# Three early moves in a gated attention and MLP kernel: a load of x onto ScalarE's queue, another load ahead of a transpose, and one key product a place later

## The chip, the cores and the metric

The kernel runs on one core of a Trainium2 chip. A core has TensorE (matrix products, in the profile PE, its weight loads PEld), VectorE (DVE), ScalarE (ACT), GpSimd (POOL) and SyncE (SP), each with an instruction stream of its own, and 16 DMA engines that all of them give work to. Products land in PSUM, eight banks of 512 float32 columns for 128 partitions. The metric is the time on the device in microseconds (us), as a median of several runs; less is better.

## The reference

x has 2048 tokens of 640 features (bfloat16). A gate mixes a linear attention block and an MLP block that both start from x:

```python
def _A_ref(x, wqkv, wo):
    H = 32; Dh = D // H
    qkv = (x @ wqkv).reshape(B, S, 3, H, Dh).transpose(2, 0, 3, 1, 4)
    q, k, v = qkv[0], qkv[1], qkv[2]
    phi = lambda t: jnp.where(t > 0, t + 1, jnp.exp(t)) + 1e-6
    pq, pk = phi(q), phi(k)
    kv = jnp.einsum("bhsd,bhse->bhde", pk, v)
    z = jnp.einsum("bhsd->bhd", pk)
    o = jnp.einsum("bhqd,bhde->bhqe", pq, kv) / (jnp.einsum("bhqd,bhd->bhq", pq, z)[..., None] + 1e-6)
    return o.transpose(0, 2, 1, 3).reshape(B, S, D) @ wo
...
g = _sigmoid((x * gate_w).sum(-1, keepdims=True))
return g * _A_ref(x, wqkv, wo) + (1 - g) * _B_ref(x, w1, w2, w3, w4)
```

`_B_ref` is a layer norm, a 640 by 640 product with GELU, shifts of the tokens by one or two, another 640 by 640 product with a residual, then a second layer norm and an MLP of width 1728 with a residual. The change touches the first stage alone, in which queries and keys are made from x.

## The kernel before, in words

The tokens are 16 tiles of 128. In the first stage each tile of x is loaded (`x_tok`), transposed into `xT`, and multiplied with the query weights `wq` and the key weights `wkg`; ScalarE takes the exponential, and VectorE makes the feature map `phi` of it (a minimum, then a `scalar_tensor_tensor` that reads the product's bank and frees it). The key product carries 130 more columns: the last key features, a column of ones, and the gate.

Instructions are recorded by `_Sched`. It keeps one program for each engine, in the order of recording, and works out the waits from what each instruction reads and writes. `sch.dma("sp", ...)` and `sch.dma("act", ...)` put a DMA into SyncE's or ScalarE's program. An engine works its program in order, so a DMA that waits holds up every later one in that program, its own data's or not.

Tiles 0 to 2 are transposed by TensorE (`t_x`), since nothing else is there to do yet. Tiles 3 to 15 are transposed by DMA: `x_turn(t)` (lines 711 and 712) is a DMA transpose in SyncE's program that waits for the load of its tile; four semaphores are used in turn for these, so turn 7 also waits for turn 3. All loads of x are in SyncE's program too (`load_x`, lines 702 and 703, and the loop at lines 735 to 738). The order there is: loads 0 and 1, one query weight block, loads 2 and 3 (3 waits for 1), turn 3, loads 4 and 5, turns 4 and 5, the load of tiles 6 to 9 as one transfer, turns 6 to 8, the load of tiles 10 to 15, turns 9 to 15. ScalarE's program has four query weight blocks, five key weight blocks (`load_wk`, one for each 128 rows) and the last 128 columns of the query weights, and then its activations.

TensorE's order in the first stage is written out by hand. `q_three` (line 950) interleaves the queries of tiles 0 to 2 with their transposes, `k_three` (line 959) does the keys of the same three tiles: its list has pairs (tile, row block), so (2, 0) is the third tile's product with the first block of 128 weight rows. One such pair is two matmuls, of 512 and 130 columns (lines 943 and 614 in the profile). `stream` issues them; each tile has its pair of PSUM banks for the whole of `k_three`, and the third tile's pair was used by a query before. Behind them each tile from 3 on has its query (`q_tile`, line 606 in the profile), its key (`k_tile`, line 625) and at times a product with all four tiles of a group (`q_turned`) or a step of a product of x and the keys (`gt_tail`). The rest of the kernel, from 54 us on, is ordered by a planner (`_Items.run`) that works with estimated times; its order of instructions and its PSUM banks are the same in both kernels.

Of the kernel before, what the change touches and what calls it, by code (L numbers as in the profile page):

```python
# [15 lines left out]
NT = S // 128  # L16
# [400 lines left out]
def _build(nc, A_x, A_wqkv, A_wo, B_w1, B_w2, B_w3, B_w4, gate_w, out, dbg=None, stop=None):  # L417
    sch = _Sched(nc)
# [54 lines left out]
    x_tok = pa.alloc("x_tok", [128, NT, D], BF16)  # L473
# [46 lines left out]
    def bank():  # L520
        best = None
        for k_ in range(nbanks[0]):
            b = (bank_rr[0] + k_) % nbanks[0]
            if b in bank_pend or b in bank_hold:
                continue
            lk = sch.locks.get(b)
            tfree = 0.0 if lk is None else sch.ev_time.get((lk[1].sem, lk[1].val), 1e18)
            if best is None or tfree < best[0]:
                best = (tfree, b)
        bank_rr[0] = best[1] + 1  # L530
        bank_pend.add(best[1])
        return best[1]
# [4 lines left out]
    def pair():  # L537
        best = None
        for k_ in range(4):
            q_ = (bank_rr[0] // 2 + k_) % 4  # L540
            tf = 0.0
            ok = True
            for b in (2 * q_, 2 * q_ + 1):
                if b in bank_pend or b in bank_hold:
                    ok = False
                lk = sch.locks.get(b)
                if lk is not None:
                    tf = max(tf, sch.ev_time.get((lk[1].sem, lk[1].val), 1e18))
            if ok and (best is None or tf < best[0]):
                best = (tf, 2 * q_)  # L550
        b = best[1]
        bank_rr[0] = b + 2
        bank_pend.update((b, b + 1))
        return b
# [3 lines left out]
    def slot(name, n):  # L558
        i = slot_ctr.get(name, 0)
        slot_ctr[name] = i + 1  # L560
        return i % n
# [49 lines left out]
    def mm_kept(e, o, l, r, start, stop, check=True):  # L611

        ll = e.lower_ap(l, for_matmul_weights=True)
        return e.add_instruction(mybir.InstMatmult(  # L614
            name=nc.get_next_instruction_name(), engine=e.engine, ins=[e.lower_ap(r), ll], outs=[e.lower_ap(o)],
            start_tensor_calc=start, stop_tensor_calc=stop, bass_skip_group_check=not check, tile_size=(128, 128),
            tile_position=(0, 0), ldweights=False))
# [23 lines left out]
    def ts(engf, out_ap, in_ap, s1, s2, op0, op1, extra_reads=()):  # L641
        rd = [in_ap] + [a for a in (s1, s2) if not isinstance(a, (int, float)) and a is not None] + list(extra_reads)
        cost = None
        if engf is pool:
            cost = 190.0 + 1.15 * nfree(out_ap)
        elif in_ap.dtype == BF16 and out_ap.dtype == BF16 and not in_psum(in_ap):
            cost = 65.0 + nfree(out_ap) / 3.84
        return engf(lambda e: e.tensor_scalar(out_ap, in_ap, s1, s2, op0, op1), rd, [out_ap], cost=cost)  # L648
# [9 lines left out]
    def stt(out_ap, in0, scalar, in1, op0, op1, accum=None):  # L658
        rd = [in0, in1] + ([scalar] if not isinstance(scalar, (int, float)) else [])
        n = nfree(out_ap)  # L660
        cost = (65.0 + n / 0.96) if (in_psum(in0) or in_psum(in1)) else (160.0 + 1.04 * n)
        if accum is not None:
            return dve(lambda e: e.scalar_tensor_tensor(out_ap, in0, scalar, in1, op0, op1, accum_out=accum), rd,  # L663
                       [out_ap, accum], cost=cost + 70.0)
        return dve(lambda e: e.scalar_tensor_tensor(out_ap, in0, scalar, in1, op0, op1), rd, [out_ap], cost=cost)  # L665
# [3 lines left out]
    def activation(out_ap, in_ap, func, scale=1.0, bias=0.0, accum=None):  # L669
        rd = [in_ap] + [a for a in (scale, bias) if not isinstance(a, (int, float))]  # L670
        wr = [out_ap] + ([accum] if accum is not None else [])
        n = nfree(out_ap)
        cost = max(150.0, 100.0 + 0.833 * n + (70.0 if in_psum(in_ap) else 0.0)) + 45.0 * (len(rd) - 1)
        if accum is not None:
            cost += 91.0
        st_ = ACT_SET.get(func)
        if st_ is not None and st_ != sch.act_func:
            cost += 1290.0
            sch.act_func = st_
        if accum is not None:  # L680
            return act(lambda e: e.activation(out_ap, in_ap, func, bias=bias, scale=scale, accum_out=accum), rd, wr, cost=cost)  # L681
        return act(lambda e: e.activation(out_ap, in_ap, func, bias=bias, scale=scale), rd, wr, cost=cost)  # L682
# [14 lines left out]
    x2 = A_x[0]  # L697

    def dma_in(out_ap, in_ap, key, **kw):
        return sch.dma("sp", out_ap, in_ap, key, **kw)  # L700

    def load_x(t, **kw):
        dma_in(x_tok[:, t, :], x2[128 * t:128 * (t + 1), :], "x%d" % t, **kw)
# [7 lines left out]
    def x_turn(t):  # L711
        sch.dma("sp", xT[:, :, 128 * t:128 * (t + 1)], x_tok[:, t, :], "trx%d" % (t % 4), transpose=True)
# [14 lines left out]
    sch.dma("act", wq[:, :, 512:D], A_wqkv[:, 512:D].rearrange("(k p) f -> p k f", p=128), "wqt")  # L727
    load_x(3, deps=[sch.dma_last["x1"]])
    sch.dma("pool", xn[0:KD, 1, 0:128], gate_w.rearrange("(k p) -> k p", p=128), "gw")
    x_turn(3)  # L730
    load_x(4)
    load_x(5)
    x_turn(4)
    x_turn(5)
    for t0, t1, turns in ((6, 10, range(6, 9)), (10, NT, range(9, NT))):
        dma_in(x_tok[:, t0:t1, :], x2[128 * t0:128 * t1, :].rearrange("(n p) d -> p n d", p=128), "xc%d" % t0)
        for t in turns:
            x_turn(t)

    k_done = {}  # L740
# [67 lines left out]
    def phi(b, dst, after_exp=None, n=D):  # L808
        se = slot("E", 3)
        src = psf[:, 512 * b:512 * b + n]  # L810
        er = Er[:, se, 0:n]
        activation(er, src, ACTF.Exp)
        if after_exp is not None:
            after_exp()
        ts(dve, er, er, 1.0, EPS_PHI, ALU.min, ALU.add)
        return stt(dst, src, 1.0 + EPS_PHI, er, ALU.add, ALU.max)
# [78 lines left out]
    def warmup(cols, cyc):  # L895
        b = bank()
        one = nc.const_aps.tensor(1.0, [128, 512], BF16)
        steps = [512] * (cols // 512) + [128] * (cols % 512 // 128)

        def fn(e):  # L900
            ins = None
            for n in steps:
                ins = e.matmul(ps[:, b, 0:n], one[:, 0:128], one[:, 0:n], start=True, stop=True)
            return ins
        pe(fn, [], [ps[:, b, :]], cost=cols * cyc)
# [19 lines left out]
    def stream(order, w, n2, done):  # L925
        bs = {}
        for t in sorted({t for t, k in order if k is not None}):
            if not n2 and t == 1:
                bank_rr[0] += 1
            bs[t] = pair() if n2 else bank()  # L930
            bank_hold.update((bs[t], bs[t] + 1) if n2 else (bs[t],))
        for t, k in order:
            if k is None:
                if t is None:
                    warmup(256, 0.42)
                else:
                    t_x(t)
                continue
            b = bs[t]
            l = xT[:, k, 128 * t:128 * (t + 1)]  # L940

            def fn(e, l=l, b=b, k=k):
                ins = e.matmul(ps[:, b, 0:512], l, w[:, k, 0:512], start=(k == 0), stop=(k == KD - 1))
                return ins if not n2 else mm_kept(e, ps[:, b + 1, 0:n2], l, w[:, k, 512:512 + n2], k == 0, k == KD - 1)
            pe(fn, [l, w[:, k, 0:512 + n2]], [ps[:, b, 0:512]] + ([ps[:, b + 1, 0:n2]] if n2 else []), cost=272.0 if n2 else 216.0)
            if k == KD - 1:
                bank_hold.difference_update((b, b + 1) if n2 else (b,))
                done(t, b)

    def q_three():  # L950
        order = [(0, 0), (1, None), (0, 1), (1, 0), (1, 1), (0, 2), (1, 2), (0, 3), (1, 3), (2, None), (0, 4), (1, 4),
                 (2, 0), (2, 1), (2, 2), (2, 3), (2, 4)]
        stream(order, wq, 0, lambda t, b: phi(b, pq_tok[:, t + 1, 0:512], n=512))

    def k_out(t, b):
        k_done[t] = phi(b, pk_tok[:, t, :], lambda: activation(lr[:, t, :], ps[:, b + 1, 128:130], ACTF.Copy))
        activation(junk[:, 0, :], x_tok[:, t, :], ACTF.Square, accum=st1[:, 1, t:t + 1])

    def k_three():
        stream([(0, 0), (1, 0), (2, 0), (0, 1), (1, 1), (0, 2), (2, 1), (1, 2), (0, 3), (2, 2), (0, 4), (1, 3), (2, 3),  # L960
                (1, 4), (2, 4)], wkg, 130, k_out)

    def addA(name, dur, fn, deps=()):
# [461 lines left out]
    for t in range(NT):  # L1425
        g = GOF[t]
        t0, t1 = GROUPS[g]
# [73 lines left out]
```

## Time and profile before

| | us |
|---|---|
| median of 3 runs | 259.33 |
| lowest, highest | 258.81, 259.79 |
| the profiled execution's own time | 259.23 |
| its span, first instruction to last | 258.0 |
| TensorE busy in it | 252.8 |
| ScalarE, VectorE, GpSimd busy | 107.3, 145.2, 91.0 |

Times in the rows are microseconds from the start of the span. In a timeline a row gives the start, the time taken, the engine, the line of the kernel (of a helper, where one records the instruction), the operation, what is written and read, how many were merged, and in brackets how long the engine had been idle and what ended that. "SPq" and "ACTq" rows are the issuing of DMAs, in SyncE's and ScalarE's programs; the transfer itself ends later, and the rows of the DMA view give the median time from issue to landing. A row of waits gives the engine, its line and what it waited for, with the sum, the count and the longest.

### The profile page before, as it was taken

To read this page: it belongs to the slowest core of one execution; us is meant where nothing else is said; L and a number is where in the kernel's file an instruction comes from. 1 tells how busy PE (TensorE), PEld (TensorE's weight loads), DVE (VectorE), ACT (ScalarE), POOL (GpSimd) and SP (SyncE) were. 2 spreads that over 40 slices of the span, in tenths; PEclk is the share of its full clock that TensorE was granted. 3 is DMA by queue.
4 is the path that set the end of the run, shared out by engine and by line. 5 is a ranking of instruction groups with operands and counts; after the bars stand their busy time and mean duration, and the time that the engine had idled before them with its cause. 6 is when DMAs were issued, how large, how long until landed. Compare 5 with 4: busy or idle time off the path is not lost.

```text
span 258.0 us, 3580 instructions
## 1 busy us (share of the span) xinstructions
PE 252.8 (98%) x1392; PEld 110.4 (43%) x1242; DVE 145.2 (56%) x290; ACT 107.3 (42%) x220; POOL 91.0 (35%) x146
## 2 busy tenths in 40 slices
PE   8998999999999999999999999999999999999997
PEld 3333343344444333334444444444444444444444
DVE  2597888899953995589999603759100033200033
ACT  2495676751356858666655600003520100253000
POOL 5021399967772153758919001223000021300000
DMA  6953799845843599462585400032100022200002
GB/s 196 236 152 80 204 172 211 213 105 127 105 101 79 97 335 381 88 103 51 127 104 125 106 10 20 0 127 53 26 0 0 20 24 101 102 1 3 0 20 102
DMA packets 57825, 26.48 MB, mean 103 GB/s; under 512 B 49188, under 2 KB 56397, under 8 KB 57808
## 3 DMA queue, kind: packets, MB, share of 16 engines
q1 hardware_dynamic: 54544, 21.38, 35.8%
q0 software_dynamic: 1168, 3.28, 5.2%
q10 hardware_dynamic: 2096, 1.61, 2.0%
q8 instruction: 10, 0.16, 0.3%
q14 instruction: 7, 0.06, 0.1%
HBM read 12.04 MB, written 2.62 MB: 57 GB/s over the span
## 4 chain that ended last, share of the span: by engine, by line
PE 89%; DMA 7%; SPq 2%; issue 1%; DVE 0%
PE ps L606 35%; PE ps L1238 30%; PE ps L625 11%; PE ps L830 7%; DMA x_tok<-in_A_x_dram 6%; PE ps L614 4%; SPq L281 1%; PE ps L1284 1%; DMA xT<-x_tok 1%; PE ps L1144 1%; PE ps L1030 0%; DVE Mt L691 0%; SPq L285 0%; PE ps L1056 0%; DVE x_tok L665 0%
## 5 line engine op out<-in xcount | busy, mean ns | idle before, releaser
L606 PE MATMUL ps<-xnT,w 128*128 128x512 bf16 x352 | 79.9, 379 | 0.5 <-issue 0.2
L665 DVE SCALAR_TENSOR_TENSOR x_tok<-ps,stg,abx 128x512 bf16<-128x512 f32 (+2 forms) x17 | 12.2, 719 | 78.4 <-PE ps L1238 78.3
L682 ACT ACTIVATE h2T<-ps 128x512 bf16<-128x512 f32 x52 | 30.7, 597 | 59.8 <-PE ps L606 59.8
L606 PEld LDWEIGHTS ps<-xnT,w 128*128 128x128 bf16 x360 | 34.6, 98 | 41.6 <-issue 1.9
L1238 PE MATMUL ps<-w,h2T 128*128 128x512 bf16 (+2 forms) x218 | 45.9, 366 | 0.3 <-issue 0.2
L648 POOL TENSOR_SCALAR xn<-x_tok,st 128x640 bf16<-128x640 bf16 x32 | 34.8, 1093 | 26.1 <-DMA xnT<-xn 25.5
L648 POOL TENSOR_SCALAR abx<-x_tok,stg 128x640 f32<-128x640 bf16 (+1 forms) x16 | 15.0, 944 | 71.2 <-DVE x_tok L665 71.2
L1238 PEld LDWEIGHTS ps<-w,h2T 128*128 128x128 bf16 x221 | 21.1, 98 | 24.1 <-issue 0.3
L682 ACT ACTIVATE Er<-ps 128x512 bf16<-128x512 f32 (+1 forms) x36 | 23.0, 651 | 16.3 <-PE ps L614 10.9
L681 ACT ACTIVATE junk<-x_tok 128x640 bf16<-128x640 bf16 x32 | 23.6, 738 | 3.9 <-DVE x_tok L663 3.7
L682 ACT ACTIVATE hsT<-ps 128x512 bf16<-128x512 f32 (+1 forms) x32 | 19.0, 594 | 13.5 <-PE ps L606 13.1
L625 PE MATMUL ps<-w,hsT 128*128 128x512 bf16 x76 | 22.3, 379 | 0.0
L663 DVE SCALAR_TENSOR_TENSOR x_tok<-ps,x_tok 128x640 bf16<-128x640 f32 x16 | 13.1, 821 | 10.7 <-PE ps L614 10.1
L1238 PE MATMUL ps<-M_sb,pqnT 128*128 128x512 bf16 (+2 forms) x83 | 18.6, 366 | 0.1
L625 PE MATMUL ps<-wkg,xT 128*128 128x512 bf16 x62 | 18.6, 379 | 0.1
L614 PE MATMUL ps<-wkg,xT 128*128 128x130 bf16 x80 | 17.6, 220 | 0.2
L830 PE MATMUL ps<-pk_tok,x_tok 128*128 128x512 bf16 x79 | 17.7, 379 | 0.1
L614 PE MATMUL ps<-w,hsT 128*128 128x128 bf16 x80 | 17.5, 219 | 0.2
L1173 DVE TENSOR_TENSOR pq_tok<-pq_tok,dnr 128x300 bf16<-128x300 bf16 (+1 forms) x48 | 17.2, 412 | 0.5
L648 DVE TENSOR_SCALAR Er<-Er 128x512 bf16<-128x512 bf16 (+1 forms) x36 | 12.3, 341 | 8.0 <-ACT Er L682 7.4
L606 PE MATMUL ps<-wq,xT 128*128 128x512 bf16 x64 | 15.9, 379 | 0.7 <-DMA xT<-x_tok 0.7
L656 DVE TENSOR_TENSOR qprod<-qprod,pk_tok 128x640 f32<-128x640 f32 x13 | 15.2, 1166 | 0.4
(91 smaller groups left out, 252.7 us busy)
## 6 DMA issues: line engine op xcount, KB each, us to landing
w<-in_B_w_dram SPq DMA_DIRECT2D x1, 2160.0 KB, 8.2
w<-in_B_w_dram SPq DMA_DIRECT2D x1, 2080.0 KB, 13.4
out_dram<-x_tok SPq DMA_DIRECT2D x3, 640.0 KB, 3.1
w<-in_B_w_dram POOLq DMA_DIRECT2D x8, 160.0 KB, 4.9
x_tok<-in_A_x_dram SPq DMA_DIRECT2D x6, 160.0 KB, 3.0
x_tok<-in_A_x_dram SPq DMA_DIRECT2D x1, 960.0 KB, 5.5
wkg<-in_A_wqkv_dram ACTq DMA_DIRECT2D x5, 160.0 KB, 3.8
wv<-in_A_wqkv_dram POOLq DMA_DIRECT2D x1, 800.0 KB, 5.2
```

What stands on the lines that cost most here:

```text
L606: ins = e.matmul(out_ap, l, r, start=(i == 0), stop=(i == n - 1))
L614: return e.add_instruction(mybir.InstMatmult(name=nc.get_next_instruction_name(), engine=e.engine, ins=[e.lower_ap(r), ll], outs=[e.lower_ ...
L625: e.matmul(outs[0], l, r, start=st, stop=sp, skip_group_check=True)
L648: return engf(lambda e: e.tensor_scalar(out_ap, in_ap, s1, s2, op0, op1), rd, [out_ap], cost=cost)
L656: return engf(lambda e: e.tensor_tensor(out_ap, a, b_, op), [a, b_], [out_ap], cost=cost)
L663: return dve(lambda e: e.scalar_tensor_tensor(out_ap, in0, scalar, in1, op0, op1, accum_out=accum), rd, [out_ap, accum], cost=cost + 70.0)
L665: return dve(lambda e: e.scalar_tensor_tensor(out_ap, in0, scalar, in1, op0, op1), rd, [out_ap], cost=cost)
L681: return act(lambda e: e.activation(out_ap, in_ap, func, bias=bias, scale=scale, accum_out=accum), rd, wr, cost=cost)
L682: return act(lambda e: e.activation(out_ap, in_ap, func, bias=bias, scale=scale), rd, wr, cost=cost)
L830: ins = e.matmul(o, l, r, start=(t0 + q_ == 0), stop=(t0 + q_ == NT - 1))
L1173: dve(lambda e, o=o, i0=i0, i1=i1: e.tensor_tensor(o, i0, i1, ALU.mult), [i0, dnr[:, 1, sd, :]], [o], cost=cost)
L1238: ins = e.matmul(o, l, r, start=first and i == 0, stop=last and i == len(prs) - 1, skip_group_check=True)
```

## The change

Three things are moved, and nothing is computed differently.

- The load of tiles 6 to 9 (640 KB) goes from SyncE's program to ScalarE's, where it is recorded behind the queries of tiles 0 to 2, that is, behind their third exponential. It has no wait there. Turns 6 to 8, the load of tiles 10 to 15 and turns 9 to 15 keep their order in SyncE's program.
- The load of tile 4 stands ahead of turn 3 in SyncE's program, right behind the load of tile 3.
- In `k_three` the pairs (2, 0) and (0, 1) change places. The wait for the second key weight block moves forward with (0, 1), the wait for VectorE moves back with (2, 0).

```diff
+    load_x(4)
     x_turn(3)
-    load_x(4)
     load_x(5)
     x_turn(4)
     x_turn(5)
-    for t0, t1, turns in ((6, 10, range(6, 9)), (10, NT, range(9, NT))):
-        dma_in(x_tok[:, t0:t1, :], x2[128 * t0:128 * t1, :].rearrange("(n p) d -> p n d", p=128), "xc%d" % t0)
-        for t in turns:
+
+    def load_xs(queue, t0, t1):
+        sch.dma(queue, x_tok[:, t0:t1, :], x2[128 * t0:128 * t1, :].rearrange("(n p) d -> p n d", p=128), "xc%d" % t0)
+
+    def late_x():
+        load_xs("act", 6, 10)
+        for t in (6, 7, 8):
+            x_turn(t)
+        load_xs("sp", 10, NT)
+        for t in range(9, NT):
             x_turn(t)
...
         stream(order, wq, 0, lambda t, b: phi(b, pq_tok[:, t + 1, 0:512], n=512))
+        late_x()
...
-        stream([(0, 0), (1, 0), (2, 0), (0, 1), (1, 1), (0, 2), (2, 1), (1, 2), (0, 3), (2, 2), (0, 4), (1, 3), (2, 3),
+        stream([(0, 0), (1, 0), (0, 1), (2, 0), (1, 1), (0, 2), (2, 1), (1, 2), (0, 3), (2, 2), (0, 4), (1, 3), (2, 3),
                 (1, 4), (2, 4)], wkg, 130, k_out)
```

## The prediction

> **What bounds the kernel now.** I read the page's head and its chain of waits first, then TensorE's waits alone, then the chain of the first 24 us, then the timeline around each place that the change touches.
>
> ```profile
> span 258.0 us, 3580 instructions
> PE 252.8 (98%) x1392; PEld 110.4 (43%) x1242; DVE 145.2 (56%) x290; ACT 107.3 (42%) x220; POOL 91.0 (35%) x146
> ...
> PE 89%; DMA 7%; SPq 2%; issue 1%; DVE 0%
> ```
>
> TensorE is busy for 98% of the span and holds 89% of the chain. The 9% of DMA and SyncE must be one early stretch, since TensorE has few waits of its own:
>
> ```profile
> PE ps L903 <- PEq L1486: 0.8, 1, 0.8
> PE ps L606 <- DMA xT<-x_tok: 0.7, 1, 0.7
> PE ps L606 <- issue: 0.2, 1, 0.2
> PE ps L1238 <- issue: 0.2, 1, 0.2
> ```
>
> The first row is the launch. The second is the only wait for another's work that is listed after it, and the chain of the first 24 us says what it was for:
>
> ```profile
> 4.31 3.60 DMA x_tok<-in_A_x_dram
> ...
> 7.93 1.30 SPq L281
> ...
> 9.28 2.98 DMA x_tok<-in_A_x_dram
> ...
> 14.86 5.77 DMA x_tok<-in_A_x_dram
> ...
> 20.64 2.37 DMA xT<-x_tok
> ...
> 23.05 1.04 PE ps L606 x4
> ```
>
> SyncE's queue works in order. It waits for tile 3 and turns it (7.93), issues tiles 4 and 5 (9.28), waits for them and turns them, and only at 14.86 issues the load of tiles 6 to 9. That lands at 20.63, tile 6 is turned by 23.01, and the query of tile 6 starts at 23.05. What TensorE loses there is read from starts, because a matmul's shown duration overlaps the next one:
>
> ```profile
> 22.14 0.22 PE L614 MATMUL ps<-x_tok,pk_tok 128*128 128x128 bf16 x1
> 23.05 1.25 PE L606 MATMUL ps<-wq,xT 128*128 128x512 bf16 x5 [0.69 <-DMA xT<-x_tok]
> ...
> 29.52 0.22 PE L614 MATMUL ps<-x_tok,pk_tok 128*128 128x128 bf16 x1
> 29.57 1.24 PE L606 MATMUL ps<-wq,xT 128*128 128x512 bf16 x5
> ```
>
> The same pair of instructions follows at 0.05 us two tiles later, and at 0.91 us here. The wait costs 0.86 us, not the 0.69 that is listed as idle.
>
> The second place is the third key tile's first product:
>
> ```profile
> 8.13 0.10 PEld L943 LDWEIGHTS ps<-wkg,xT 128*128 128x128 bf16 x1 [0.15 <-DMA wkg<-in_A_wqkv_dram]
> 8.31 0.38 PE L943 MATMUL ps<-wkg,xT 128*128 128x512 bf16 x1
> 8.33 0.69 DVE L665 SCALAR_TENSOR_TENSOR pq_tok<-ps,Er 128x512 bf16<-128x512 f32 x1
> ...
> 8.58 0.38 PE L943 MATMUL ps<-wkg,xT 128*128 128x512 bf16 x1
> ...
> 9.07 0.33 PEld L943 LDWEIGHTS ps<-wkg,xT 128*128 128x128 bf16 x2 [0.45 <-DVE pq_tok L665]
> 9.08 0.39 PE L943 MATMUL ps<-wkg,xT 128*128 128x512 bf16 x1
> 9.36 0.38 PE L943 MATMUL ps<-wkg,xT 128*128 128x512 bf16 x1
> ```
>
> Products of this stage start 0.27 apart (8.31, 8.58). The third should start at 8.85 and starts at 9.08, because its bank is freed by VectorE at 9.02 (8.33 + 0.69). This loss is 0.23 us.
>
> **The change, part by part.** *The load of tiles 6 to 9* leaves SyncE's queue, and with it the waits for tiles 3, 4 and 5. It is issued by ScalarE behind three exponentials, without a wait of its own.
>
> ```profile
> 7.37 1.73 ACT L682 ACTIVATE Er<-ps 128x512 bf16<-128x512 f32 x3 [3.19 <-PE ps L943]
> 11.74 0.70 ACT L682 ACTIVATE Er<-ps 128x640 bf16<-128x640 f32 x1 [2.64 <-PE ps L614]
> 14.86 0.58 SPq L285 DMA_DIRECT2D x_tok<-in_A_x_dram  x1
> 16.17 1.24 PE L606 MATMUL ps<-wq,xT 128*128 128x512 bf16 x5
> ```
>
> ScalarE is free at 9.10 and next needed at 11.74. One issue of this load took SyncE 0.58, so it ends near 9.7, inside the 2.64 idle: cost nothing. Queued behind it on ScalarE is the first key's exponential, on which VectorE and then TensorE's banks wait; without that idle it would cost up to its 0.58. By its own 5.77 the load lands near 14.9 instead of 20.63. SyncE's queue before turn 6 then holds the load of tile 5 at 9.28 and turns 4 and 5, the latter from about 12.3 (9.28 + 2.98). Turn 6 goes at about 14.9 and lands 2.37 later, at 17.3, against 22.19 where TensorE wants it (22.14 + 0.05). Even with a further 1.2 us (two 160 KB loads in front of it, at the rate in the rows below) the margin is over 3 us. The load of tiles 10 to 15 stays on SyncE behind turn 8, so it moves forward with it. The 0.86 us is gone: I take all of it.
>
> *Tile 4 ahead of turn 3.* SyncE issues it when it is done with tile 3's load, at 4.64 instead of 9.28, and so in the middle of the key weights, which ScalarE issues from 4.57 on:
>
> ```profile
> 2.18 2.46 SPq L285 DMA_DIRECT2D x_tok<-in_A_x_dram  x2
> 4.57 2.27 ACTq L285 DMA_DIRECT2D wkg<-in_A_wqkv_dram  x5
> ...
> 7.00:8.00 1.00, 1.00 (x6) 0.42 (x5) 0.64 (x4) 0.63 (x2) 0.00 (x0) 1.00 1.02 323
> 8.00:9.00 1.00, 1.00 (x7) 0.19 (x2) 0.96 (x3) 0.95 (x2) 0.00 (x0) 1.00 0.79 252
> ...
> 12.00:13.00 1.00, 1.00 (x8) 0.45 (x5) 0.49 (x2) 1.00 (x3) 0.00 (x0) 1.00 0.03 9
> ```
>
> The columns behind the clock are the DMA engines' share and GB/s. From 7 to 9 us they are full or nearly so, so 160 KB more there push what is behind them by 0.5 (323 GB/s) to 0.63 us (252). Who is behind them is seen from the issues, each asked for in its own stretch: the second key weight block (issued at 5.02, 4.57 and a fifth of 2.27) and turn 3 (7.93).
>
> ```profile
> wkg<-in_A_wqkv_dram ACTq DMA_DIRECT2D x1, 160.0 KB, 3.5
> xT<-x_tok SPq DMA_TRANSPOSE x1, 3.8
> ```
>
> The second block landed at 8.52 (5.02 + 3.5). The first, whose row reads the same, landed at 8.07 (4.57 + 3.5), and 8.13 shows its wait ending with TensorE at its own pace of 0.27 behind it, so there is little to spare, but whatever this delays is counted once with the second block's delay.
>
> *The order of the key products.* The second product of tile 0 now stands third, and needs the second block; the one that waits for VectorE stands fourth, at 9.12 at the earliest, behind 9.02. Undisturbed, the second block is there at 8.52, the third product starts at 8.85 and 0.23 is gained. Pushed by 0.63 it lands at 9.15 and is used at 9.21 (the first block's 0.06 from landing to weight load), 0.13 after 9.08: a loss of 0.13. Tile 4 follows tile 3 on SyncE's queue, tile 3 landed at 7.91 (4.31 + 3.60), and so tile 4 takes only a share of the engines before the second block is through. I take a push of 0.4 us: start 8.98, gain 0.10. The ends, -0.13 and +0.23, go into the range.
>
> The Trainium skill, "DMA: Bandwidth & Descriptors", section "Queues, rings and completion order", has each DMA engine take turns, packet by packet, between the queues that have work. By that alone tile 4 would get half of the engines until it is through, and the sum would move by less than the two ends just given.
>
> *Turn 3* landed at 11.73 (7.93 + 3.8) and is first used here:
>
> ```profile
> 12.58 0.80 PEld L606 LDWEIGHTS ps<-wq,xT 128*128 128x128 bf16 x5 [0.17 <-issue]
> ...
> 24.53 0.58 SPq L285 DMA_DIRECT2D x_tok<-in_A_x_dram  x1
> 25.16 1.24 SPq L281 DMA_TRANSPOSE xT<-x_tok  x1
> ...
> xT<-x_tok SPq DMA_TRANSPOSE x1, 6.2
> ```
>
> It has 0.85 us to spare. With weights pushed into it by 0.4 to 0.63 it still comes in time. But the 640 KB now start behind 9.10, while it is under way. The dearest turn of the trace is tile 9's, issued at 25.16 right behind the load of tiles 10 to 15 (960 KB) on its own queue: 6.2 us, the last row. At that price turn 3 lands at 14.13, 1.55 late. The 640 KB are on another queue, behind the last key and query weights, so I stay near the 3.8 and take 0.05 as a mean loss; 0 and 1.55 are the ends. Turn 4 goes at 9.86 (9.28 and an issue of 0.58), and even at 6.2 lands at 16.06, against 16.17.
>
> *What moves later.* VectorE's and GpSimd's instructions, banks and order are the same in both kernels, and behind 23.05 TensorE waits for nobody by the list above. So a shift at 23 us arrives at the end whole.
>
> *Sum:* 0.86 + 0.10 - 0.05 = 0.91 us. The profiled execution took 259.23 us for its span of 258.0. That gives 258.32, and 258.42 from the median of 259.33, which is 0.10 above the profiled one. I say **258.4**.
>
> **Rivals.**
>
> *A, everything at its best:* the second block isn't pushed, 0.86 + 0.23 = 1.09, 258.2. For it: from 8 to 9 us the engines are at 0.79, not full. Against it: 1.02 the microsecond before.
>
> *B, the gain is eaten by the weights:* tile 4 pushes the blocks by the full 0.63 (loss 0.13), and turn 3, pushed by that and by a part of the 640 KB, comes some 0.4 late: 0.86 - 0.53 = 0.33, 259.0. For it: 0.85 is all that turn 3 has.
>
> *C, slower:* turn 3 is crowded as tile 9's was. From 0.85 us of delay on it costs TensorE its excess, from 1.71 on (0.85 + 0.86) it costs more than the change saves, and at 6.2 us it is 1.55 late. With the weights' 0.13 that is 0.86 - 1.68 = -0.82, so 260.1; to pass 260.6 it would have to land 0.5 later still. For it: its data flow while the DMA engines are at their fullest. Against: the large load has a queue of its own here, and stands in it behind 960 KB of weights.
>
> *D, no difference:* the load is issued earlier, but shares the engines so long that tile 6 comes no earlier. Then 0.86 stays lost, and with the order's 0.10 less turn 3's 0.05 the time is 259.3. Against it speaks the window from 12 to 13 us, with the engines at 0.03: there is room for 640 KB before 15 us, and the load was late for its issue's sake. The Trainium skill, "DMA: Bandwidth & Descriptors", section "Rules for kernel authors", says so of every such move: spreading loads over several issuing engines gives no bandwidth, since all run on the same 16 DMA engines, and saves only issue time. The trace agrees that the engines are shared, but the time between 9.3 and 14.86 was spent in SyncE's queue.
>
> **How the numbers follow.** Forecast 0.55, A 0.25, B 0.10, C 0.05, D 0.05. Three runs of before lie from 258.81 to 259.79, so a median moves by some 0.4 either way. Forecast and A with that reach from 257.8 to 258.9, and B and D to 259.4: the range is **257.7 to 259.4**, with C and half of D's upper side left out. About 0.5% (1.3 us, 258.03 and 260.63) is what a measurement of this kernel tells from no change. The forecast stands 0.4 on the slow side of the lower bound, A 0.2: a sixth of the one and a half of the other give 0.09 + 0.13 = 0.22 for faster. Slower takes C whole and a little for what I haven't seen: 0.06. Same is the rest, 0.72.
>
> **What would show it.** TensorE's wait for the turned tile at line 606 is gone, and the load of tiles 6 to 9 stands on ScalarE's queue near 9.1 with turn 6 issued by about 16. The third key product starts between 8.85 and 9.21, and waits for key weights, if for anything. The query of tile 3 follows its key products at 0.05; a wait for the turned tile there is C or B. VectorE's bank wait (9.07) is gone or small. I am wrong if the query of tile 6 still waits, if a new wait on TensorE behind 23 us takes the gain back, or if the three places are as said and the span isn't 0.7 to 1.1 shorter.

## The result, and the profile after

| | before | after |
|---|---|---|
| median, us | 258.94 | 260.88 |
| lowest, highest | 258.49, 259.79 | 258.88, 265.51 |
| runs | 22 | 22 |
| ratio, 95% interval | | 1.0055 (1.0035 to 1.0076) |
| profiled execution's own time | 259.23 | 263.71 |
| its span | 258.0 | 262.5 |

The change makes the kernel slower by 0.35 to 0.76%, and it makes it unsteady: the runs of before lie within 1.3 us, those of after within 6.6. The profiled execution is one of two in 22 in which TensorE's mean granted clock is below 1 (0.993 here; 0.987 in the run of 265.51), and the ratio leaves these two out; a second profile of the same kernel, with a whole clock, follows in the experiments.

The head of the profile's page after, and the chain's shares by engine:

```profile
span 262.5 us, 3580 instructions
PE 254.7 (97%) x1392; PEld 110.7 (42%) x1242; DVE 145.3 (55%) x290; ACT 107.5 (41%) x220; POOL 90.9 (35%) x146
...
PE 92%; DMA 6%; issue 1%; DVE 0%; SPq 0%
```

TensorE still bounds the kernel, but 7.8 us of the span are now without it (262.5 - 254.7), where it was 5.2. TensorE's waits after say for what:

```profile
PE ps L606 <- DMA xT<-x_tok: 3.2, 1, 3.2
PE ps L910 <- PEq L1494: 0.8, 1, 0.8
```

One wait at the same line as before, for a turned tile, but more than four times as long (3.2 against 0.7). The chain of the first 30 us after (start, length, what) says that it is another tile:

```profile
4.49 3.79 DMA x_tok<-in_A_x_dram
8.30 8.03 DMA xT<-x_tok
16.37 1.46 PE ps L606 x5
```

The load of tile 3 ends at 8.28, its turn is issued at 8.30 and lands 8.03 later, at 16.33. So it is turn 3 that the query of tile 3 waits for, not turn 6 any more. The timeline after, with the engines concerned (line 950 of the changed kernel is line 943 of the one before):

```profile
8.15 0.29 DVE L648 TENSOR_SCALAR Er<-Er 128x512 bf16<-128x512 bf16 x1 [0.32 <-ACT Er L682]
8.30 1.29 SPq L281 DMA_TRANSPOSE xT<-x_tok  x1
7.52 1.77 ACT L682 ACTIVATE Er<-ps 128x512 bf16<-128x512 f32 x3 [3.33 <-PE ps L950]
8.70 0.39 ACTq L285 DMA_DIRECT2D x_tok<-in_A_x_dram  x1
...
8.65 0.33 PEld L950 LDWEIGHTS ps<-wkg,xT 128*128 128x128 bf16 x2 [0.50 <-DMA wkg<-in_A_wqkv_dram]
8.94 0.38 PE L950 MATMUL ps<-wkg,xT 128*128 128x512 bf16 x1
9.49 0.33 PEld L950 LDWEIGHTS ps<-wkg,xT 128*128 128x128 bf16 x2 [0.51 <-DMA wkg<-in_A_wqkv_dram]
9.49 0.39 PE L950 MATMUL ps<-wkg,xT 128*128 128x512 bf16 x1
...
12.89 0.33 DVE L648 TENSOR_SCALAR Er<-Er 128x640 bf16<-128x640 bf16 x1 [1.87 <-ACT Er L682]
12.99 0.22 PE L614 MATMUL ps<-wkg,xT 128*128 128x130 bf16 x1
16.37 1.46 PE L606 MATMUL ps<-wq,xT 128*128 128x512 bf16 x5 [3.16 <-DMA xT<-x_tok]
17.63 0.63 PE L625 MATMUL ps<-wkg,xT 128*128 128x512 bf16 x1
18.16 0.63 PE L625 MATMUL ps<-wkg,xT 128*128 128x512 bf16 x1
```

The query of tile 3 should follow the last key product by 0.05, at 13.04, and starts at 16.37: 3.33 us lost. Behind that its key products stand 0.53 apart instead of 0.27. The windows after (length, busy time of the five engines, granted clock, DMA share, GB/s) show why:

```profile
17.30:20.70 3.40, 3.40 (x13) 0.91 (x7) 0.99 (x2) 0.75 (x2) 0.00 (x0) 0.50 0.74 101
20.70:24.00 3.30, 3.25 (x19) 1.31 (x14) 2.53 (x6) 2.41 (x6) 1.91 (x5) 1.00 0.51 107
```

For 3.4 us the granted clock is 0.50, which costs an estimated 1.7 us, half of that stretch. In the first stage, then, the bill against the profile of before reads as follows. The first query's minimum on VectorE starts at 8.15; before, this row and that of the first key stood so (the timeline of before):

```profile
8.00 0.29 DVE L648 TENSOR_SCALAR Er<-Er 128x512 bf16<-128x512 bf16 x1 [0.36 <-ACT Er L682]
12.48 0.33 DVE L648 TENSOR_SCALAR Er<-Er 128x640 bf16<-128x640 bf16 x1 [1.60 <-ACT Er L682]
...
26.80 0.82 DVE L665 SCALAR_TENSOR_TENSOR pk_tok<-ps,Er 128x640 bf16<-128x640 f32 x1
```

So 0.15 is late at the first query (8.15 - 8.00), 0.26 is lost between the two minima (12.89 - 8.15 = 4.74 instead of 4.48), 3.33 in the wait for turn 3, 1.70 by the half clock, and 0.86 is won back, since tile 6 has no wait: 4.58, and the span is longer by 4.5. The same product of VectorE that starts at 26.80 above starts 4.49 later after:

```profile
31.29 0.82 DVE L665 SCALAR_TENSOR_TENSOR pk_tok<-ps,Er 128x640 bf16<-128x640 f32 x1
```

From there to the end of the span the shift stays 4.5 us. All that happened did so in the first 26 us.

Where the 8 us of turn 3 went is seen in the DMA view after. Asked for in their own stretch, the issues of ScalarE's load and of turn 3 (KB, us to landing), and behind them the queues' packets that began from 9 to 10 us, from 10 to 11 and from 13 to 14 (packets, MB, share of 16 engines):

```profile
x_tok<-in_A_x_dram ACTq DMA_DIRECT2D x1, 640.0 KB, 7.7
xT<-x_tok SPq DMA_TRANSPOSE x1, 8.0
...
q10 hardware_dynamic: 467, 0.34, 103.5%
...
q10 hardware_dynamic: 483, 0.15, 80.8%
q1 hardware_dynamic: 241, 0.06, 28.0%
...
q10 hardware_dynamic: 199, 0.25, 82.7%
q1 hardware_dynamic: 199, 0.05, 27.8%
```

q10 carries what ScalarE issues, q1 what SyncE issues. From 9 to 10 us, behind its issue at 8.30, turn 3 has no packet at all; the weights of ScalarE's queue run. From 10 to 11 it gets 241 of its 640 (160 KB in packets of 256 bytes). The rest runs beside the 640 KB. From 13 to 14 us the two queues got 199 packets each, but a packet of the load has 1280 bytes and one of a transpose 256: 0.25 MB went to the load and 0.05 to SyncE's queue, with the turn for which TensorE was standing still. The equal count is that of this one microsecond; from 11 to 12 it was 71 to 121, from 14 to 15 163 to 264.

### The profile page after: what moved, and what is told of

Its sections match the earlier page's. It is cut to its first block, busy times and chain, and to the rows that moved or that the text cites. A ratio compares the mean times of both kernels' runs of the same rounds, so it can differ in the third digit from the quotient of the medians.

```text
span 262.5 us, 3580 instructions
## 1 busy us (share of the span) xinstructions
PE 254.7 (97%) x1392; PEld 110.7 (42%) x1242; DVE 145.3 (55%) x290; ACT 107.5 (41%) x220; POOL 90.9 (35%) x146
## 4 chain that ended last, share of the span: by engine, by line
PE 92%; DMA 6%; issue 1%; DVE 0%; SPq 0%
PE ps L606 37%; PE ps L1246 30%; PE ps L625 13%; PE ps L837 7%; PE ps L614 4%; DMA xT<-x_tok 3%; DMA x_tok<-in_A_x_dram 3%; PE ps L1292 1%; PE ps L1152 1%; PE ps L1038 0%; DVE Mt L691 0%; SPq L285 0%; PE ps L1064 0%; DVE x_tok L665 0%
## 5 line engine op out<-in xcount | busy, mean ns | idle before, releaser
L625 PE MATMUL ps<-wkg,xT 128*128 128x512 bf16 x62 | 19.9, 399 | 0.1
```

Of the source, the lines that this page charges most:

```text
L625: e.matmul(outs[0], l, r, start=st, stop=sp, skip_group_check=True)
```

## The experiments

The theory is that the second queue does the harm: on ScalarE's queue the 640 KB run beside turn 3 and take every other packet, where on SyncE's they would stand behind it. The first rival is that tile 4's early load, and with it the key weights, crowd turn 3. A second is that the amount alone matters, wherever it is issued. Where the expectations use letters, L and O are the theory, W is the first rival and E the second. Diffs are against the changed kernel, those of no_load, order_only and the last pair against the kernel before, that of pool_tile4_back against pool_after_turn3. All medians stand beside those of before that were measured with them:

| kernel | median (range), us | before | ratio (95%) |
|---|---|---|---|
| load_only | 259.17 (258.62 to 262.54) | 259.06 | 1.0026 (1.0000 to 1.0052) |
| no_load | 259.04 (258.66 to 259.55) | 259.06 | 1.0004 (0.9992 to 1.0015) |
| order_only | 259.06 (258.60 to 259.84) | 259.06 | 1.0001 (0.9990 to 1.0013) |
| pool_after_turn3 | 259.17 (258.61 to 259.68) | 259.06 | 1.0004 (0.9992 to 1.0015) |
| own_queue_gone | 259.06 (258.81 to 259.42) | 259.08 | 1.0005 (0.9996 to 1.0014) |
| act_tile6_only | 259.21 (259.04 to 259.62) | 259.08 | 1.0009 (0.9999 to 1.0020) |
| pool_tile4_back | 259.81 (259.25 to 260.00) | 259.08 | 1.0032 (1.0021 to 1.0043) |
| tile6_alone | 258.75 (258.13 to 259.41) | 259.08 | 0.9991 (0.9981 to 1.0002) |
| act_tiles6_7 | 259.59 (258.75 to 260.67) | 259.16 | 1.0016 (1.0002 to 1.0030) |
| tile6_old_order | 258.85 (258.59 to 259.00) | 259.16 | 0.9989 (0.9979 to 0.9998) |

**The parts alone.** *load_only* is the change without tile 4's move and without the key products' order:

```diff
-    load_x(4)
     x_turn(3)
+    load_x(4)
...
-        stream([(0, 0), (1, 0), (0, 1), (2, 0), (1, 1), (0, 2),
+        stream([(0, 0), (1, 0), (2, 0), (0, 1), (1, 1), (0, 2),
```

> Only the load of tiles 6 to 9 is moved to ScalarE's queue; tile 4's load and the key order are as before. Theory L (the 640 KB run on a queue of their own beside turn 3 and hold it up): turn 3 takes over 5.5 us from issue to landing, TensorE's query of tile 3 waits 1 to 3.5 us for it, and the time is 259.5 to 263 with a wide spread from run to run. Rival W (tile 4's early 160 KB push the weights and turn 3; the large load is harmless): turn 3 lands within 4.5 us, no wait there, tile 6's wait is gone, and the time is 258.1, which is 0.86 under the kernel before.

Most of its runs are as before, but 4 of 12 lie above 260 (260.07, 260.49, 260.75, 262.54), and none of before does. The profiled one (258.62) is the shortest. Its timeline and its DMA view:

```profile
8.98 0.42 ACTq L285 DMA_DIRECT2D x_tok<-in_A_x_dram  x1
...
x_tok<-in_A_x_dram ACTq DMA_DIRECT2D x1, 640.0 KB, 4.8
xT<-x_tok SPq DMA_TRANSPOSE x1, 3.4
```

Turn 3 was issued at 7.60 here, 0.7 earlier than after, and took 3.4; no wait at tile 3 is listed. So the profile is as W expected and the spread as L did, and neither foresaw the median. That the load alone does the harm in the four long runs is likely, but none of them has a profile. With tile 4 ahead of turn 3 long runs are the rule: 15 of 22 of the changed kernel are above 260.

*no_load* is the other half, tile 4's move and the order, with the 640 KB left on SyncE's queue:

```diff
+    load_x(4)
     x_turn(3)
-    load_x(4)
...
-        stream([(0, 0), (1, 0), (2, 0), (0, 1), (1, 1), (0, 2),
+        stream([(0, 0), (1, 0), (0, 1), (2, 0), (1, 1), (0, 2),
```

> Tile 4's load ahead of turn 3 and the new key order, but the load of tiles 6 to 9 stays on SyncE's queue. Theory L: turn 3 lands within 4.8 us, the query of tile 3 waits under 0.3 us, tile 6's wait at about 23 us is as before, and the time is within 0.3 us of the kernel before. Rival W: the query of tile 3 waits 1 us or more and the time is 260 or more.

No loss: tile 4 and the weights alone don't make turn 3 late, and the first rival falls. There is no gain either, although its profile shows no wait at tile 6, where the theory had expected one.

*order_only* has the new order of the key products and nothing else of the change.

```diff
-        stream([(0, 0), (1, 0), (2, 0), (0, 1), (1, 1), (0, 2),
+        stream([(0, 0), (1, 0), (0, 1), (2, 0), (1, 1), (0, 2),
```

> Only the key order is changed. Both theories: the third key product starts 0.27 us behind the second in place of 0.50, the keys of the first three tiles end 0.2 us earlier. Since the wait for tile 6 comes behind that and is set by loads that don't move, theory L and rival W both expect the gain to be eaten by that wait: time equal to the kernel before within 0.2 us.

The third product stands at TensorE's pace, and the time is that of before to the hundredth. Its profile still shows the wait at tile 6 (0.84).

**The queue.** *pool_after_turn3* is the whole change, but with the load issued by GpSimd once turn 3 has landed:

```diff
-        load_xs("act", 6, 10)
+        load_xs("pool", 6, 10, deps=[sch.dma_last["trx3"]])
```

> The whole change, but the load of tiles 6 to 9 is issued by GpSimd, which waits for turn 3's landing first. Theory L: turn 3 lands within 4.8 us of its issue, no wait of 0.3 us or more at the query of tile 3, the load lands by 20 us, tile 6's wait is gone, and the time is 258.0 to 258.4, with the narrow spread of the kernel before. Rival W: the wait at the query of tile 3 stays at 1 us or more, and the time is 260 or more.

Turn 3 took 4.5 us, and neither tile 3 nor tile 6 waited. The harm is gone, but the gain that I expected with it did not come. The query of tile 6 starts at 22.86 here; in the two profiles of before it starts at 23.05 with a wait and, as shown below, at 22.36 without one.

*own_queue_gone* keeps the moment and takes away only the second queue: the 640 KB stand on SyncE's queue right behind turn 3, ahead of tile 5.

```diff
-    load_x(5)
-    x_turn(4)
-    x_turn(5)
...
-        load_xs("act", 6, 10)
+        load_xs("sp", 6, 10)
+        load_x(5)
+        x_turn(4)
+        x_turn(5)
```

> The whole change, but the 640 KB stay on SyncE's queue, right behind turn 3 and ahead of tile 5's load, so they are issued at about the same moment (near 9.5 us) as in the changed kernel. Theory O (what hurts is the second queue: on one queue turn 3's packets all stand ahead of the load's): turn 3 lands within 4.8 us of its issue and TensorE's query of tile 3 waits under 0.3 us; the price moves to turns 4 and 5, which now stand behind 800 KB. Rival E (what hurts is 640 KB starting on the same engines at that moment, whatever the queue): turn 3 takes over 5.5 us and the query of tile 3 waits 1 us or more, as in the changed kernel.

This one sets the theory against the amount. Its timeline and its DMA view, with the packets of its SyncE queue from 10 to 11 and from 11 to 12 us behind:

```profile
9.57 1.13 SPq L285 DMA_DIRECT2D x_tok<-in_A_x_dram  x2
13.10 1.24 PE L606 MATMUL ps<-wq,xT 128*128 128x512 bf16 x5
...
x_tok<-in_A_x_dram SPq DMA_DIRECT2D x1, 640.0 KB, 4.8
xT<-x_tok SPq DMA_TRANSPOSE x1, 3.9
...
q1 hardware_dynamic: 399, 0.10, 113.2%
...
q1 hardware_dynamic: 298, 0.17, 93.0%
```

The same 640 KB are issued while turn 3 (8.21 here) is still under way, on the same 16 engines, and turn 3 takes 3.9 us; the query of tile 3 starts without idle time (a wait would stand in brackets). Up to 11 us the queue's packets are the turn's (0.10 MB in 399 of them, some 256 bytes each), and the load's larger ones follow. Its runs lie within 0.61 us. So the amount alone does no harm, and the second rival falls. What this run doesn't separate is the queue from the distance: its load was issued 1.36 us behind turn 3, after only 0.40 (8.70 - 8.30), and load_only, 1.38 behind on ScalarE's queue, had a turn 3 of 3.4 us. A load behind the turn in one queue keeps that order; with two queues the order can turn out either way. Turn 4, which stands behind the 640 KB here, took 4.8 us and still came in time.

*pool_tile4_back* is pool_after_turn3 with tile 4 back behind turn 3.

```diff
-    load_x(4)
     x_turn(3)
+    load_x(4)
```

> The load of tiles 6 to 9 issued by GpSimd behind turn 3's landing, the new key order, but tile 4 loaded at the old place. Beside the same kernel with tile 4 early this shows what tile 4's early load costs: if the key weights it pushes are 0.2 to 0.3 us late, this one is 0.2 to 0.3 us faster than that one, 258.7 to 258.9; if tile 4's place is free, both are equal.

This missed, and why it did supports the theory. Its timeline and its DMA view:

```profile
11.72 0.86 POOL L285 DMA_DIRECT2D x_tok<-in_A_x_dram  x1 [6.99 <-DMA xT<-x_tok]
17.52 1.25 PE L606 MATMUL ps<-wq,xT 128*128 128x512 bf16 x5 [1.01 <-DMA xT<-x_tok]
...
x_tok<-in_A_x_dram POOLq DMA_DIRECT2D x1, 640.0 KB, 5.1
xT<-x_tok SPq DMA_TRANSPOSE x1, 4.9
```

Turn 4, now issued at 12.57 because tile 4 is loaded later, runs beside the load on GpSimd's queue, takes 4.9 us where turns alone take 2.4 to 2.5, and the query of tile 4 waits for 1.01 us. It is the same collision one turn later, from another engine's queue. What tile 4's early load costs can't be read from this time.

**The amount on the second queue.** *act_tile6_only* puts only tile 6 (160 KB) on ScalarE's queue, *act_tiles6_7* tiles 6 and 7 (320 KB); the rest follows on SyncE's behind it.

```diff
-        load_xs("act", 6, 10)
+        load_xs("act", 6, 7)
+        load_xs("sp", 7, 10)
```

> The whole change, but ScalarE's queue carries tile 6 alone (160 KB), and tiles 7 to 9 (480 KB) stay on SyncE's queue behind turn 5. If turn 3 is held up by the amount that runs beside it packet by packet, a quarter of the amount leaves it within 5 us and the query of tile 3 waits under 0.4 us, time 258.6 to 259.3. If it is held up by the start of any load on the other queue, turn 3 still takes over 5.5 us in the profile or the runs still spread to 260 and more.

> The whole change, but ScalarE's queue carries tiles 6 and 7 (320 KB); tiles 8 and 9 stay on SyncE's queue behind turn 5. Between 160 KB there (no run above 259.62, no wait at the query of tile 3) and the change's 640 KB (median 260.9, up to 265.5). Theory L (turn 3 is held up by the amount that runs beside it on the other queue): in between, some runs at 259.6 to 260.5, median 259.2 to 259.7. Rival (only the last part of the 640 KB, or their later landing, does it): the time and spread of the 160 KB kernel, median under 259.2.

The diff is act_tile6_only's; the other has `8` in place of `7`. In the profiles turn 3 took 4.1 us beside 160 KB and 4.8 beside 320, both without a wait at tile 3; the medians go 259.21, 259.59 and, with all 640 KB, 260.88, the highest runs 259.62, 260.67 and 265.51. The times fit that more on the second queue makes a late turn 3 more frequent and later, but no profile of these two shows a late one. Nor does the amount alone differ: the load's issue came 0.08 us behind turn 3's in one profile (8.84 - 8.76) and 1.70 in the other (9.30 - 7.60).

**A wait that isn't always there.** *before_again* and *after_again* are one more profile of either kernel, unchanged.

> The kernel before once more, for a second profile. If the wait for tile 6 absorbs a late start of TensorE, then the query of tile 6 starts at about the same 23 us, and its wait is smaller where VectorE's first query work (8.00 in the first profile) is later. If the wait is a fixed cost, it is 0.7 to 0.9 again whatever the start.

> The changed kernel once more, for a second profile. Theory L: the query of tile 3 waits for turn 3 again, by another amount (0.5 to 3.5 us), turn 3 takes over 5 us, the load of tiles 6 to 9 runs beside it, and behind the first 26 us nothing differs from the kernel before but the shift. A second profile without that wait and yet a time of 260 or more would refute it.

before_again took 258.53 with a span of 257.3. Its timeline at the key products and at tile 6, and its DMA view:

```profile
8.70 0.38 PE L943 MATMUL ps<-wkg,xT 128*128 128x512 bf16 x1
...
9.25 0.38 PE L943 MATMUL ps<-wkg,xT 128*128 128x512 bf16 x1
...
22.30 0.22 PE L614 MATMUL ps<-x_tok,pk_tok 128*128 128x128 bf16 x1
22.36 1.24 PE L606 MATMUL ps<-wq,xT 128*128 128x512 bf16 x5
...
x_tok<-in_A_x_dram SPq DMA_DIRECT2D x1, 640.0 KB, 4.4
```

The 640 KB landed in 4.4 us instead of 5.77, and the query of tile 6 follows at 0.06: the 0.86 that the change was to win isn't there. The other two kernels with the load at its old place agree: order_only, where it took 5.9, has the wait, and no_load, where it took 4.5, has none. The recorded expectation looked to a late start of TensorE for this; it is the load's own time that differs. Nor is the key products' 0.23: the first product starts at 8.70 instead of 8.31, and the third follows at pace, because by then VectorE has freed its bank.

after_again took 260.52 with a span of 259.3. Its timeline and its DMA view:

```profile
9.11 0.60 ACT L682 ACTIVATE Er<-ps 128x512 bf16<-128x512 f32 x1 [0.28 <-PE ps L950]
9.12 0.41 ACTq L285 DMA_DIRECT2D x_tok<-in_A_x_dram  x1
13.40 0.22 PE L614 MATMUL ps<-wkg,xT 128*128 128x130 bf16 x1
14.85 1.25 PE L606 MATMUL ps<-wq,xT 128*128 128x512 bf16 x5 [1.23 <-DMA xT<-x_tok]
...
x_tok<-in_A_x_dram ACTq DMA_DIRECT2D x1, 640.0 KB, 5.5
xT<-x_tok SPq DMA_TRANSPOSE x1, 6.0
```

Turn 3 takes 6.0 us and costs 1.40 (14.85 - 13.45). The clock stays whole. Its time is near the kernel's median, so this is nearer to its usual case.

**A version without the second queue.** *tile6_alone* loads tile 6 alone behind tile 5, and tiles 7 to 9 at the old place, all on SyncE's queue, with the new order of the key products; *tile6_old_order* is that with the old order. The diff is the latter's:

```diff
     load_x(5)
+    load_x(6)
     x_turn(4)
     x_turn(5)
-    for t0, t1, turns in ((6, 10, range(6, 9)), (10, NT, range(9, NT))):
+    for t0, t1, turns in ((7, 10, range(6, 9)), (10, NT, range(9, NT))):
```

> The kernel before with the new key order, and tile 6 loaded alone behind tile 5 on SyncE's queue; tiles 7 to 9 stay at the old place, tile 4 too. Nothing new runs beside turn 3, and tile 6 is there by 15 us. If the wait for tile 6 is worth what the profile says, its 0.86 us less what TensorE's early stage varies by from run to run, the time is 258.2 to 258.7, under the kernel before. If early variation eats it (the wait only absorbs a late start), the time is within 0.2 us of the kernel before.

> Tile 6 loaded alone behind tile 5 on SyncE's queue, as in the best kernel so far, but with the key order of before. If the order is worth its 0.23 us once no wait for tile 6 follows, this one is 0.1 to 0.25 us slower than the one with the new order, 258.85 to 259.0. If the order's gain is lost elsewhere in the early stage, both are equal within 0.1 us.

Neither profile shows a wait at tile 3, 4 or 6. tile6_old_order is faster than before by 0.11% (0.02 to 0.21), the only kernel of the ten whose interval lies below 1, and barely; tile6_alone is within its spread. Their ratios, 0.9989 and 0.9991, are as good as equal, so the key products' order is worth nothing that shows. An estimate of what the wait at tile 6 costs over many executions is the difference of the medians, about 0.3 us (259.16 - 258.85, and 259.08 - 258.75), not 0.86; by the interval of tile6_old_order anything from 0.05 to 0.54 would do.

## Why the prediction was wrong

*What bounds the kernel, and that shifts arrive whole,* was right: from 26 us on everything stands 4.5 us later, as the end does.

*Turn 3* is the step that failed. It was given 3.8 us, with 0.05 as its term of the sum, because "the 640 KB are on another queue, behind the last key and query weights, so I stay near the 3.8". Neither half gave the shelter that was meant. Another queue was taken for a shelter and is the opening: own_queue_gone shows turn 3 at 3.9 us with the load behind it on its own queue, and the two profiles after show 6.0 and 8.0 us with the load on ScalarE's, issued 0.28 and 0.40 us behind the turn. The prediction had cited the rule for this, from the Trainium skill, "DMA: Bandwidth & Descriptors", section "Queues, rings and completion order", that an engine takes turns between queues by packets, and weighed it for tile 4's load and the weights alone. The 199 and 199 packets of one microsecond fit it; the counts around it are uneven, so the taking of turns itself is not shown here. The row should have been turned round: tile 9's 6.2 us was a turn behind 960 KB in one queue, which says nothing of what two queues do. Nor was 6.2 an upper end, since turn 3 took 8.0.

The other half, that the load stands behind the weights, held and did not help. Its issue began at 8.70, while the third exponential was still running (7.52 + 1.77 = 9.29), and not behind it at 9.10; yet the load's first packets run only from about 10.3 us on. But turn 3 waits behind the same weights: tile 3 landed 0.37 later than before (8.28 against 7.91), and by 11 us the turn had 241 of 640 packets through. In load_only it was issued at 7.60 and had landed by 11.0 (7.60 + 3.4), when the load had hardly begun: 91 packets of its queue ran from 10 to 11 us. What decides, by these profiles, is which of the two gets to the engines first, and the prediction compared times of issue and landing, not those in which the packets run.

*Rival C*, given a chance of 0.05, is what happened: turn 3 crowded, a wait for the turned tile in the query of tile 3, and the excess over 0.85 us paid. Its price for turn 3 was right for a light case: 1.55 expected, 1.40 in after_again, 3.33 in the first profile; its 260.1 still counted the 0.86 as won. The half clock behind the long wait, 1.7 us, was in no case of mine. *Rival B* had the two right places, the weights and turn 3, at less than a third of their price (0.53 against 0.45 and 1.40 in after_again); *A*'s 0.23 wasn't there to be won.

*The load's gain at tile 6* was right in its mechanism, for the wait is gone, and too large by a factor of nearly three: 0.86 was read from one execution in which the 640 KB had taken 5.77 us. With 4.4 there is no wait to remove. The medians of the last pair say about 0.3.

*Tile 4 and the key products' order* were given +0.10, between -0.13 and +0.23. The named mechanism came, a push of the weight blocks, but larger: after, the first block is late for TensorE (0.50 of idle, the weight load at 8.65), and the third product waits for the second one until 9.49 instead of 9.21. From the first query's minimum to the first key's it takes 4.48 and 4.47 in the two profiles of before, 4.74 and 4.92 in those after: 0.26 and 0.45 lost. In no_load, with the load off the scene, this stretch takes 4.73 (8.70 to 13.43), and in order_only, without tile 4's move, 4.46 (8.06 to 12.52), so it is tile 4's 160 KB. The other profiles agree: the seven with tile 4 early have 4.61 to 5.15, the seven with it at its old place 4.23 to 4.48. This is a part of why the kernels with tile 4 early show no gain even where no turn is late. The lower bound of -0.13 was no bound, because it pushed only the second block. The 0.23 on the other side was a wait that the second profile of before does not have, and order_only gained nothing.

*Rival D* was wrong for this kernel: the load did land early enough that tile 6 had no wait. The rule of the Trainium skill behind it, "DMA: Bandwidth & Descriptors", section "Rules for kernel authors", that issuing from several engines gives no more bandwidth, is not contradicted; the turn paid for what the load got.

One sum behind the range is off by 0.1: the forecast with its 0.4 reaches 258.8, not 258.9. The range doesn't depend on it, since its upper end comes from B and D.

With the terms as they were measured, the second pair of profiles comes out: 0.21 late at the first query (8.38 - 8.17), 0.45 at the keys, 1.40 at turn 3, nothing won at tile 6, together 2.06, and the spans differ by 2.0 (259.3 - 257.3).

What stays open: how near behind the turn, on another queue, the load may start without harm (0.28 and 0.40 us did harm, 1.38 did none in the one profile), and why the load's and the turn's packets were so slow around 12 us in the first profile after. From 12.0 to 12.5 us both queues together moved 14 GB/s:

```profile
12.00:12.50 0.50, 1.00 0.31 14
...
13.00:13.50 0.50, 1.00 1.03 279
```

The columns of these windows of the first profile after are the length, the granted clock, the DMA share and GB/s. That two queues share the engines explains why the turn gets a part; it doesn't explain why for a microsecond nobody gets much, which may be the difference between the 6.0 and the 8.0. A slow start of this load is seen without any turn beside it, too: in the first profile of before it moved 100 GB/s from 16 to 17 us, at a DMA share of 0.79, and 320 GB/s in the next microsecond, at 0.89. So turn 3 may have met the load's slow start as much as its amount; no run tells the two apart.

## What to carry to other kernels

A load that is moved to another engine's queue leaves the order of the old queue as well as its waits: it can run beside whatever is critical there, and here, at equal counts of packets, its larger ones took five times the bytes. A bulk load is safer behind the critical transfer, in the same queue or with a wait for its landing; or it is split so that only what is needed next goes ahead (tile 6 alone did no harm and may have kept a gain of 0.3 us). And a wait that one profile shows is worth its length only if a second profile shows it too: here 0.86 and 0.23 us, credited from one execution, were both absent from the next.

## What the runs showed of the hardware

- A DMA that stands behind an activation in ScalarE's program begins to issue while the activation runs: at 8.70 beside one that ended at 9.29, and at 9.12 beside one of 0.60 us that had begun at 9.11.
- The same 640 KB took 4.4, 5.77, 4.8, 5.5 and 7.7 us from issue to landing in five profiles, with 4.4 and 5.77 from one kernel and 5.5 and 7.7 from the other.
- A wait of 3.16 us on TensorE was followed by 3.4 us at a granted clock of 0.50, which began 0.93 us after the wait's end (17.30 - 16.37); one of 1.23 us by none. The Trainium skill, "TensorE: Matmul & The Clock Gate", section "Part 1: The HAM clock gate (the "warmup" mystery)", has the clock halve after an idle window of about 3.4 us and return after a busy one of that length. The trace agrees with the second figure; the wait was a little shorter than the first.
